# Writing a chunk's residual early, and dropping the join at a chunk's end, in a delta-rule attention and two-MLP kernel

## The chip, the cores and the metric

The kernel runs on one core of a Trainium2 chip. The metric is the device time of one execution in microseconds (us); lower is better.

## The reference

Three parts run one after the other, for 4 batches of 768 tokens.

```python
# 1: attention with the delta rule, 8 heads of 48
k_n = k / (np.linalg.norm(k, axis=-1, keepdims=True) + 1e-06)
for t in range(S):
    y[:, :, t] = einsum('bhd,bhde->bhe', q[:, :, t], state)
    v_old = einsum('bhde,bhd->bhe', state, k_n[:, :, t])
    state = state + beta * einsum('bhd,bhe->bhde', k_n[:, :, t], v[:, :, t] - v_old)
# 2: mixing over tokens, then an MLP (384 -> 1536 -> 384)
u = x + (x.transpose(0, 2, 1) @ U @ V).transpose(0, 2, 1)
x1 = u + np.maximum(u @ w_ch1, 0) @ w_ch2
# 3: 2-D Fourier transform, normalisation, a second MLP of the same size
u = x1 + real(fft(fft(x1, axis=1), axis=2))
out = u + np.maximum(normalise(u) @ w_ch1, 0) @ w_ch2
```

## The kernel before, in words

Attention works on 24 chunks ("units"): 4 batches of 6 chunks of 128 tokens, all 8 heads together. A chunk's own triangular system is prepared without knowing the state (`s_front`, `s_turn`, `s_prep_a`, `s_split`, `s_prep_b`, `s_prep_c`; the last one ends with the copy of the inverse, `nf<-ps_n`). Then `s_solve` walks the chunks in order, since each needs the state that the chunk before left. Within a chunk it writes the scaled values `vt` into the PSUM tile `R` (called `res` in the profile; ScalarE at L1087 or VectorE at L1089), adds state times keys to it with 16 matmuls (`res<-Sst,...`, L1055), and solves in three rounds, each of which reads `R` (`rh<-res`, L1068 or L1070). After the third read come `Ul` (L1121), the state update (`ps_s<-Uh,kb` and so on; `S`, L1135), the copies of the state to two fp16 halves (`Sst`, through L244 and L1145), and the chunk's output (40 matmuls into `ps_s`, then L1142, which overwrites `vt`). At the end stands a join, and the next chunk's write of `R` comes after it. In a batch's first chunk the state is zero and its matmuls are left out.

`s_mixed` adds a finished chunk's output into `hu` (`ps_hu`, L1026) and stores it. `s_mix` builds the first MLP's input once a batch's six chunks are done, with three tiles each for a block of 384 tokens (L1317, L1319, and a transposing DMA at L1338). `s_mlp` is the MLP: `ps_h` (L1190) and `acc` (L1226). The weights arrive as 64-bit numbers, are turned to fp32 on VectorE (L293, L296, L300) and split into two fp16 parts (L365 and L368). Parts 3 and the second MLP follow in `second`, once attention is done; `fold` there prepares the transform's input on GpSimd (L251) and ScalarE (L1451).

No engine chooses at run time: each works through its own list in order. These lists are made beforehand by the planner `Weave`, which keeps a clock for each engine, takes the cost that every step declares, and always issues the step with the smallest sum of earliest start and bias. A step may name two engines, of which the planner takes one by end time with a price on its duration. `PR0` and `MB0` are biases until the first batch's attention is done, `PR`, `MB`, `WB1` those after it, `P2` those of the last part; a more negative bias goes earlier. `MB0` belongs to `s_mix` up to its first finished block, `WB1` to the weights. `UP` is the number of units in which a sum of two matrices is made by one more matmul with the identity (L900) instead of an addition on VectorE. `HB` decides when the small part of an MLP's hidden value is made by a matmul with the identity (L1204) instead of VectorE (L1209). Real waits are semaphores; the planner's join only makes its own clock wait.

Of the kernel before, what the change touches and what calls it, by code (L numbers as in the profile page):

```python
# [15 lines left out]
ALU = mybir.AluOpType  # L16
# [17 lines left out]
NV = 2  # L34
AGE0 = -5
AGE = 16
EPS0 = -1085
FILL = 47
EPS = -309
UP = 13  # L40
UE = 0
NP = 27
GATE = 3
UA = 8
SPARE = 270
SPW = 120
PR0 = (-337, -112, -95, -78, -360, -173, -425, 225)
PR = (-41, -98, -140, -142, 118, 51, -956, -408)
ME = -78
MX = -401  # L50
MB = -515
MB0 = -564
P2 = (-467, -323, -887, -360, -372, -386, -1140, -392)
MP = 39
HB = -550
WB1 = -575
WB = -15
PRICE0 = {'p': 1.0, 'v': 1.45, 'a': 0.71, 'g': 0.38}
PRICE = {'p': 1.0, 'v': 0.29, 'a': 0.22, 'g': 0.14}
PRICE2 = {'p': 1.0, 'v': 283.18, 'a': 3.3, 'g': 1.14}  # L60
SC = 16.0
CQ, CV, CW, CF = 6, 10, 9, 9
CU = 5
# [8 lines left out]
class Weave:  # L72
# [66 lines left out]
    def run(self, streams, until=None):  # L139

        for s in streams:
            if not s.started:
                s.started = True
                self.step(s, None)
        while True:
            if all(s.req is None for s in streams[:until]):
                return
            best, posted, aged, fill = None, len(self.mark), [], []
            first = {}
            for s in streams:  # L150
                if s.req is None:
                    continue
                c = self.pick(s)
                if c is not None and s.fill is not None:
                    fill.append((c, s))
                elif c is not None:
                    rank = c[0] + s.bias[c[2] == "p"] + (self.aging * (s.age - self.oldest) if s.age is not None else 0.0)
                    first[c[2]] = min(first.get(c[2], 1e18), c[0])
                    if best is None or rank < best[0]:
                        best = rank, c, s  # L160
                    if s.age is not None:
                        aged.append((s.age, rank, c, s))
            if len(self.mark) > posted:
                continue
            for c, s in sorted(fill, key=lambda x: x[0][0]):
                if best is None or c[0] <= best[1][0] + 200.0 and c[0] + c[1] <= first.get(c[2], 1e18) + s.fill:
                    best = c[0], c, s
                    break
            assert best is not None, [s.req for s in streams]
            if best[2].age is not None:  # L170
                near = [x for x in aged if x[0] < best[2].age and x[2][2] == best[1][2] and x[1] < best[0] + self.window]
                if near:
                    best = min(near, key=lambda x: x[:2])[1:]
            _, (t, ns, e, mode, x), s = best
            end = t + ns
            self.free[e] = end
            if x in "wg":
                self.port = end
            if mode == "chain":
                s.main, s.par = {e: end} if ns else dict(s.par), {}  # L180
            elif mode == "par":
                s.par[e] = max(s.par.get(e, 0.0), end)
            elif len(s.req) == 3:
                self.dma = max(self.dma, end + self.FETCH) + s.req[2]
                d = {"dma": s.par, "sidedma": s.side, "late": s.late}[mode]
                d["x"] = max(d.get("x", 0.0), self.dma + self.LAND - self.LAT)
            else:
                s.side = {e: end}
            self.step(s, e)
# [8 lines left out]
def _v(n, rate=1):  # L198
    return 67 + n / (0.96 * rate)


def _a(n, psum=False):
    return (51 if psum else 93) + n / 1.2
# [10 lines left out]
class Builder:  # L214
# [822 lines left out]
    def s_solve(self):  # L1037
# [25 lines left out]
        def part(tag):  # L1063

            t = f16t(tag)
            e = yield {"a": _a(n, True), "v": _v(n)}
            if e == "a":
                nc.scalar.activation(out=t, in_=R, func=ACTF.Copy, scale=-1.0 / SC)  # L1068
            else:
                nc.vector.tensor_scalar(out=t, in0=R, scalar1=-1.0 / SC, scalar2=None, op0=ALU.mult)  # L1070
            return t

        def inverse(tag, x):
            ps = work()
            yield from hmm(ps, [(lambda h: Nf[:, h, :], x)])
            t = f16t(tag)
            yield from self.cp(t, ps, n, "chain", psum=True)
            return t

        for u, (b, c) in self.each():  # L1080
            yield ("v", u)
            yield ("scl", b)
            up, sv = self.scl[b]
            vt = self.vt[u]
            e = yield {"a": _a(n) + 94, "v": _v(n)}
            if e == "a":
                nc.scalar.activation(out=R, in_=vt, func=ACTF.Copy, scale=up)  # L1087
            else:
                nc.vector.tensor_scalar(out=R, in0=vt, scalar1=up, scalar2=None, op0=ALU.mult)  # L1089
            yield ("s", u)  # L1090
            un = self.un[u]
            dn = self.ap2.tile([128, 1], F32, tag="dn", name="dn")
            yield {"v": 130}, "par"
            nc.vector.tensor_scalar(out=dn, in0=sv, scalar1=un["sq1"], scalar2=-(2.0 ** -CV), op0=ALU.mult, op1=ALU.mult)
            yield ("c", u)
            yield ("al", 4 * u + 3)
            KT, K2, GPh, GPl, Nf, kb16 = un["KT"], un["K2"], un["GPh"], un["GPl"], un["Nf"], un["kb16"]

            def rest(x):
                return hmm(R, [(lambda h: GPh[:, h, 0:128], x), (lambda h: GPl[:, h, 0:128], x)], [(self.ids, x)],  # L1100
                           start=False)

            if c:
                yield from hmm(R, [(lambda h: KT[:, 0, h, :], St), (lambda h: K2[:, 0, h, :], St)], start=False)
            Rh = yield from part("rh")
            U0 = yield from inverse("U0", Rh)
            yield from rest(U0)
            Rh = yield from part("rh")
            d1 = yield from inverse("d1", Rh)
            yield from rest(d1)  # L1110
            ps = work()
            yield from hmm(ps, [], [(self.id16, U0), (self.id16, d1)], mode="side", stop=False)
            Uh = f16t("Uh")
            yield {"w": _v(n, 2)}, "side"
            nc.vector.tensor_tensor(out=Uh, in0=U0, in1=d1, op=ALU.add)
            Rh = yield from part("rh")
            yield from hmm(ps, [(lambda h: Nf[:, h, :], Rh)], start=False)
            yield "join"
            Ul = f16t("Ul")
            yield {"v": _v(n)}  # L1120
            nc.vector.tensor_tensor(out=Ul, in0=ps, in1=Uh, op=ALU.subtract)  # L1121
            terms = [(lambda h: GPh[:, h, 128:256], Uh), (lambda h: GPl[:, h, 128:256], Uh)]
            if c > 0:
                terms += [(lambda h: KT[:, 1, h, :], St), (lambda h: K2[:, 1, h, :], St)]
            terms.append((lambda h: GPh[:, h, 128:256], Ul))
            if c < NC - 1:
                ps = work()
                yield from hmm(ps, [(lambda h: kb16[:, h, 0, :], Uh), (lambda h: kb16[:, h, 1, :], Uh),
                                    (lambda h: kb16[:, h, 0, :], Ul)], m=64)
                yield {"v": _v(n)}  # L1130
                if c == 0:
                    S32 = self.ap2.tile([64, H, D], F32, tag="S32", name="S32", bufs=1)
                    nc.vector.tensor_scalar(out=S32, in0=ps[0:64], scalar1=1.0 / SC, scalar2=None, op0=ALU.mult)
                else:
                    nc.vector.scalar_tensor_tensor(out=S32, in0=ps[0:64], scalar=1.0 / SC, in1=S32, op0=ALU.mult, op1=ALU.add)  # L1135
            ps = work()
            yield from hmm(ps, terms, mode="side")
            if c < NC - 1:
                St = self.ap2.tile([128, H, D], F16, tag="Sst", name="Sst")
                yield from self.cp(St[0:64], S32, n, "chain")  # L1140
            yield {"a": _a(n, True) + 94}, "side"
            nc.scalar.activation(out=vt, in_=ps, func=ACTF.Copy, scale=dn)  # L1142
            if c < NC - 1:
                yield {"w": _v(n)}
                nc.vector.tensor_tensor(out=St[64:128], in0=S32, in1=St[0:64], op=ALU.subtract)  # L1145
            yield "join"
            self.wv.post("sol", u)
            self.wv.oldest = u + 1

# [603 lines left out]
```

## Time and profile before

| what | before |
|---|---|
| median of 3 runs | 1037.67 us (1035.9 to 1040.18) |
| profiled execution | 1041.91 us, its span 1039.8 us |
| busy share of the span | PE 88%, VectorE 70%, ScalarE 53%, GpSimd 34% |
| mean granted TensorE clock | 0.939 |

PE is TensorE's matmuls, PEld its weight loads, DVE is VectorE, ACT ScalarE, POOL GpSimd, SP the queue that issues most DMAs. A row such as `L1068 ACT ACTIVATE rh<-res` is line 1068 on ScalarE, writing `rh` from `res`. What stands in brackets behind a row of the timeline is the idle time of that engine ahead of the instruction and what ended it.

### The profile page before, as it was taken

The page shows a single profiled execution, that of the slowest core. Times are in us where ns is not written, and L with a number is a line of the kernel's source. Part 1 is how long each engine was busy: PE and PEld are TensorE (multiplying, and loading weights), DVE is VectorE, ACT ScalarE, POOL GpSimd, SP SyncE. Part 2 cuts the span into 40 slices and gives each one's busy share as a digit, 9 for nine tenths or more (in the row PEclk, how much of TensorE's full clock was granted, in tenths as well). Part 3 has the DMA queues.
Part 4 walks back from the last instruction along what each step waited for, and adds up shares of the span by engine and source line. Part 5 has one row for each costly group of instructions (what it writes and reads, how often), then busy time and mean ns, then how long its engine had stood idle before and what let it go on. Part 6 is the DMA issues. An engine that isn't in the chain of part 4 may idle for free. (4 is left out here: it accounts for less than half of the span.)

```text
span 1039.8 us, 25511 instructions
## 1 busy us (share of the span) xinstructions
PE 913.1 (88%) x10282; PEld 622.6 (60%) x10282; DVE 724.9 (70%) x1664; ACT 548.6 (53%) x1358; POOL 352.2 (34%) x330
## 2 busy tenths in 40 slices
PE   3465777589999899999999879999999999999998
PEld 2344665356777666676676546655756665655655
DVE  6898889898898998998765367765735554444532
ACT  5665676767777766667655244447723232222221
POOL 3554244213444323454110360046555532012010
PEclk8575989589999999999999989999999999999999
DMA  6996677316756565543502546522211311202110
GB/s 189 224 219 163 160 183 174 78 39 146 152 133 162 105 151 112 142 109 79 114 25 70 164 105 192 130 87 71 35 54 50 95 28 54 69 24 61 58 34 23
DMA packets 158253, 110.87 MB, mean 107 GB/s; under 512 B 117484, under 2 KB 146424, under 8 KB 158136
## 3 DMA queue, kind: packets, MB, share of 16 engines
q1 hardware_dynamic: 155688, 102.01, 40.6%
q0 software_dynamic: 2448, 7.24, 2.5%
q8 instruction: 80, 1.31, 0.5%
q14 instruction: 37, 0.30, 0.1%
HBM read 55.63 MB, written 14.16 MB: 67 GB/s over the span
## 5 line engine op out<-in xcount | busy, mean ns | idle before, releaser
L1226 PE MATMUL acc<-w2s,hh 128*128 128x384 f16 x1152 | 281.8, 326 | 4.9 <-DVE u L1624 3.1
L1190 PEld LDWEIGHTS <-w1s 128*128 128x128 f16 x1728 | 163.5, 98 | 114.5 <-issue 14.7
L1196 ACT ACTIVATE hh<-ps_h 128x384 f16<-128x384 f32 x192 | 93.7, 488 | 205.6 <-PE ps_h L1190 201.8
L251 POOL TENSOR_TENSOR GPl<-g,GPh 128x512 f16<-128x512 f32 x92 | 116.1, 1262 | 235.1 <-ACT GPh L244 174.2
L1209 DVE SCALAR_TENSOR_TENSOR hl<-ps_h,hh 128x384 f16<-128x384 f32 x147 | 81.6, 555 | 161.6 <-ACT hh L1196 155.8
L1226 PE MATMUL acc<-w2s,hl 128*128 128x384 f16 x576 | 188.1, 327 | 0.2 <-DVE hl L1209 0.2
L1190 PE MATMUL ps_h<-u,w1s 128*128 128x384 f16 x864 | 169.6, 329 | 11.9 <-DVE hl L1209 10.5
L1190 PE MATMUL ps_h<-uh,w1s 128*128 128x384 f16 x864 | 157.9, 327 | 0.0
L1226 PEld LDWEIGHTS <-hh 128*128 128x128 f16 x1152 | 106.2, 98 | 64.8 <-issue 8.0
L902 PEld LDWEIGHTS <-bd 128*128 128x128 f16 x1728 | 71.6, 99 | 45.7 <-issue 18.6
L1226 PEld LDWEIGHTS <-hl 128*128 128x128 f16 x576 | 56.2, 98 | 38.2 <-DVE hl L1209 0.6
L841 DVE TENSOR_TENSOR g<-ps_g,mask 128x512 f32<-128x512 f32 x96 | 65.6, 683 | 12.1 <-PE ps_g L835 11.0
L834 PE MATMUL ps_g<-KT,BT 128*128 128x256 f16 x192 | 54.0, 301 | 10.0 <-ACT t L993 5.0
L244 ACT ACTIVATE GPh<-g 128x512 f16<-128x512 f32 x75 | 47.0, 626 | 28.0 <-DVE g L841 27.3
L251 POOL TENSOR_TENSOR pair<-x1f,pair 128x384 f16<-128x384 f32 x24 | 22.2, 925 | 111.8 <-ACT pair L1594 106.8
L251 POOL TENSOR_TENSOR pm<-xq 97x768 f32<-97x768 f32 (+1 forms) x16 | 29.3, 1850 | 79.5 <-DMA xq<-x1d 72.1
L835 PE MATMUL ps_g<-K,BT 128*128 128x256 f16 x192 | 54.6, 305 | 1.9 <-DMA K<-KT 1.8
L1068 ACT ACTIVATE rh<-res 128x384 f16<-128x384 f32 x63 | 30.5, 484 | 20.0 <-PE res L1055 10.2
L902 PE MATMUL lanes<-R,bd 128*128 128x32 f16 x768 | 34.7, 179 | 4.5 <-ACT R L244 2.9
L882 DVE TENSOR_TENSOR bd<-Xc,mmask 128x1024 f16<-128x1024 f16 x48 | 34.2, 712 | 5.9 <-ACT Xc L936 5.5
L1055 PEld LDWEIGHTS <-GPh 128*128 128x128 f16 x768 | 30.2, 98 | 9.7 <-issue 6.7
L251 POOL TENSOR_TENSOR kb<-kq,rb 128x384 f32<-128x384 f32 x21 | 18.2, 867 | 50.8 <-DVE rb L658 10.9
(270 smaller groups left out, 1866.6 us busy)
## 6 DMA issues: line engine op xcount, KB each, us to landing
wst<-in_moe_w_ch_dram SPq DMA_DIRECT2D x51, 384.0 KB, 3.4
K<-KT SPq DMA_DIRECT2D x46, 256.0 KB, 3.9
kq<-in_k_dram SPq DMA_DIRECT2D x24, 192.0 KB, 3.8
kq<-in_q_dram SPq DMA_DIRECT2D x24, 192.0 KB, 4.2
vt<-in_v_dram SPq DMA_DIRECT2D x24, 192.0 KB, 2.9
xnd<-vt SPq DMA_DIRECT2D x24, 192.0 KB, 3.5
xn<-xnd SPq DMA_DIRECT2D x24, 192.0 KB, 3.0
x1d<-u SPq DMA_DIRECT2D x24, 192.0 KB, 1.9
```

The costliest lines, as they stand in the source:

```text
L244: self.nc.scalar.activation(out=out, in_=in_, func=ACTF.Copy)
L251: (self.nc.vector if eng == "v" else self.nc.gpsimd).tensor_tensor(out=out, in0=in0, in1=in1, op=op)
L834: nc.tensor.matmul(o, BT[:, h, :], KT[:, :, h, :], start=i == 0, stop=False, skip_group_check=True)
L835: nc.tensor.matmul(o, BT[:, h, :], K2[:, :, h, :], start=False, stop=True, skip_group_check=True)
L841: nc.vector.tensor_tensor(out=g32.rearrange("p i (a t) -> p (i a) t", a=2), in0=ps.rearrange("p i (a t) -> p (i a) t", a=2), in1=self.mask ...
L882: self.nc.vector.tensor_tensor(out=dst.rearrange("p h (j c) -> p h j c", j=n), in0=x, in1=mask[:, None, :, :].to_broadcast(shape), op=ALU. ...
L902: nc.tensor.matmul(ps[:, h, :], lhs[:, h, :], rhs[:, h, :], start=plus is None, stop=plus is None or h == H - 1)
L1068: nc.scalar.activation(out=t, in_=R, func=ACTF.Copy, scale=-1.0 / SC)
L1190: nc.tensor.matmul(ps[:, i, :], w[:, k, fs], u[x][:, k, :], start=(m == 0), stop=(m == 3 * KD - 1))
L1196: nc.scalar.activation(out=hh, in_=ps, func=ACTF.Relu, scale=1.0 if wi else 1.0 - 2.0 ** -11)
L1209: nc.vector.scalar_tensor_tensor(out=hl, in0=ps, scalar=0.0, in1=hh, op0=ALU.max, op1=ALU.subtract)
L1226: nc.tensor.matmul(acc, h[:, ds_], w, start=(f == 0 and j == 0), stop=(f == KF - 1 and j == 2))
```

## The change

The write of `R` for the next chunk becomes a function `first`. `s_solve` issues it right after `Ul` of the running chunk, if the planner's clock already has the next chunk's values and scale; otherwise it stays where it was. The join moves from a chunk's end to the place after the first read of the next chunk's `R`. The planner gets a kind of step ("late", without a DMA) whose end only a join waits for. About thirty of the planner's numbers change too.

```diff
-EPS0 = -1085
+EPS0 = -1123
-UP = 13
+UP = 15
-SPW = 120
+SPW = 167
-PR0 = (-337, -112, -95, -78, -360, -173, -425, 225)
-PR = (-41, -98, -140, -142, 118, 51, -956, -408)
-ME = -78
-MX = -401
-MB = -515
-MB0 = -564
-P2 = (-467, -323, -887, -360, -372, -386, -1140, -392)
+PR0 = (-337, -266, -95, -78, -360, -189, -429, 241)
+PR = (-41, -98, -140, -167, 118, 38, -1050, -459)
+ME = -57
+MX = -389
+MB = -494
+MB0 = -626
+P2 = (-467, -323, -722, -360, -372, -386, -1054, -392)
-HB = -550
-WB1 = -575
-WB = -15
-PRICE0 = {'p': 1.0, 'v': 1.45, 'a': 0.71, 'g': 0.38}
+HB = -620
+WB1 = -585
+WB = -12
+PRICE0 = {'p': 1.0, 'v': 1.45, 'a': 0.71, 'g': 0.27}
-PRICE2 = {'p': 1.0, 'v': 283.18, 'a': 3.3, 'g': 1.14}
+PRICE2 = {'p': 1.0, 'v': 446.37, 'a': 7.92, 'g': 0.8}
...
+            elif mode == "late" and len(s.req) == 2:
+                s.late[e] = max(s.late.get(e, 0.0), end)
...
+        def first(u, mode):
+
+            up = self.scl[self.units[u][0]][0]
+            e = yield {"a": _a(n) + 94, "v": _v(n)}, mode
+            if e == "a":
+                nc.scalar.activation(out=R, in_=self.vt[u], func=ACTF.Copy, scale=up)
+            else:
+                nc.vector.tensor_scalar(out=R, in0=self.vt[u], scalar1=up, scalar2=None, op0=ALU.mult)
+
+        ready = None
         for u, (b, c) in self.each():
-            yield ("v", u)
-            yield ("scl", b)
-            up, sv = self.scl[b]
+            if u != ready:
+                yield ("v", u)
+                yield ("scl", b)
+                yield from first(u, "chain")
+            sv = self.scl[b][1]
             vt = self.vt[u]
-            e = yield {"a": _a(n) + 94, "v": _v(n)}
-            if e == "a":
-                nc.scalar.activation(out=R, in_=vt, func=ACTF.Copy, scale=up)
-            else:
-                nc.vector.tensor_scalar(out=R, in0=vt, scalar1=up, scalar2=None, op0=ALU.mult)
...
             Rh = yield from part("rh")
+            yield "join"
             U0 = yield from inverse("U0", Rh)
...
             nc.vector.tensor_tensor(out=Ul, in0=ps, in1=Uh, op=ALU.subtract)
+            if u + 1 < len(self.units):
+                keys = ("v", u + 1), ("scl", self.units[u + 1][0])
+                if all(self.wv.mark.get(x, 1e18) <= self.wv.free["p"] for x in keys):
+                    for x in keys:
+                        yield x
+                    yield from first(u + 1, "late")
+                    ready = u + 1
...
-            yield "join"
             self.wv.post("sol", u)
```

## Rows read from the trace of the kernel before

**Rows 1.** Windows by stage: span, busy us of each engine, granted clock, DMA.
```profile
103.00:182.00 79.00, 57.57 (x1229) 48.23 (x1226) 70.63 (x156) 54.00 (x143) 30.03 (x29) 0.90 0.71 171
182.00:216.00 34.00, 19.94 (x204) 13.82 (x205) 29.08 (x66) 25.42 (x56) 8.46 (x8) 0.55 0.34 77
216.00:575.00 359.00, 341.42 (x5377) 248.95 (x5374) 301.58 (x670) 245.95 (x619) 114.06 (x98) 1.00 0.49 110
720.00:1040.00 320.00, 308.78 (x2009) 192.64 (x2006) 151.68 (x382) 95.53 (x223) 98.19 (x94) 0.99 0.19 51
```

**Rows 2.** Timeline, all engines, chunk 1 to chunk 2: start us, duration us.
```profile
114.37 0.49 PE L1055 MATMUL ps_s<-Ul,GPh 128*128 128x48 f16 x8
...
115.38 0.58 ACT L1087 ACTIVATE res<-vt,sup 128x384 f32<-128x384 f32 x1
...
116.13 0.36 PE L1055 MATMUL res<-Sst,KT 128*128 128x48 f16 x8
```

**Rows 3.** Timeline, all engines, chunk 2 to chunk 3.
```profile
130.41 0.51 ACT L244 ACTIVATE Sst<-S 64x384 f16<-64x384 f32 x1
...
131.93 0.54 DVE L1145 TENSOR_TENSOR Sst<-S,Sst 64x384 f16<-64x384 f32 x1
...
134.55 0.59 ACT L244 ACTIVATE nf<-ps_n 64x512 f16<-64x512 f32 x1
...
135.20 1.49 PE L1026 MATMUL ps_hu<-UU,vt 128*128 128x32 f32 x6 [0.49 <-ACT nf L244]
...
136.50 0.51 PE L1055 MATMUL res<-Sst,KT 128*128 128x48 f16 x8
```

**Rows 4.** Timeline, all engines, chunk 3 to chunk 4.
```profile
150.05 0.55 DVE L1145 TENSOR_TENSOR Sst<-S,Sst 64x384 f16<-64x384 f32 x1
...
151.11 0.36 PE L1055 MATMUL res<-Sst,KT 128*128 128x48 f16 x8
```

**Rows 5.** Timeline, all engines, chunk 4 to chunk 5.
```profile
168.36 0.58 ACT L244 ACTIVATE nf<-ps_n 64x512 f16<-64x512 f32 x1
...
170.27 0.36 PE L1055 MATMUL res<-Sst,KT 128*128 128x48 f16 x8
```

**Rows 6.** Timeline of ScalarE after the first batch's attention.
```profile
198.73 0.60 ACT L1317 ACTIVATE xn<-u,few 128x384 f16<-128x384 f32 x1
...
203.48 0.61 ACT L365 ACTIVATE w1s<-wf,few 128x384 f16<-128x384 f32 x1 [0.53 <-DVE w2s L368]
204.00 0.60 ACT L1317 ACTIVATE xn<-u,few 128x384 f16<-128x384 f32 x1
```

**Rows 7.** Timeline of SP's queue in the same stretch.
```profile
199.00 7.67 SPq L1338 DMA_TRANSPOSE u<-xn  x3
```

**Rows 8.** Timeline of TensorE in the same stretch.
```profile
210.80 1.13 PE L1190 MATMUL ps_h<-u,w1s 128*128 128x384 f16 x3
...
216.51 0.27 PE L900 MATMUL lanes<-R,id 128*128 128x256 f16 x1 [0.23 <-ACT R L244]
216.62 0.35 PE L902 MATMUL lanes<-R,bd 128*128 128x32 f16 x8
```

**Rows 9.** Line 900, one of its two groups of sums.
```profile
L900 PE MATMUL lanes<-Nc,id x26: 269/273/421, 34.2 to 307.2; 128*128 128x256 f16 x26
```

**Rows 10.** Line 1204.
```profile
L1204 PE MATMUL ps_h<-hh,idm x45: 322/323/337, 216.9 to 550.2; 128*128 128x384 f16 x45
```

**Rows 11.** Timeline, all engines, after attention's end.
```profile
600.49 0.94 ACT L1451 ACTIVATE fs<-pm,few 97x772 f16<-97x772 f32 x1 [8.96 <-POOL pm L251]
...
603.48 3.04 PE L1190 MATMUL ps_h<-u,w1s 128*128 128x384 f16 x9 [8.15 <-DVE hl L1209]
```

**Rows 12.** Timeline of SP's queue, the load of chunk 3's values.
```profile
124.97 1.20 SPq L806 DMA_DIRECT2D vt<-in_v_dram  x1
```

**Rows 13.** The same load's line: from issue to landing.
```profile
DMA to landing us min/median/max: 2.4/2.9/3.4
```

**Rows 14.** Waits of SP's queue: total us, times, longest us.
```profile
SPq L806 <- PE lanes L902: 13.2, 10, 4.5
```

## The prediction

> **What bounds the kernel now.** I read the busy shares by slice first, then the same by stage. From about 216 us on TensorE is the bound: it is busy 341.42 of 359 us up to attention's end and 308.78 of 320 us in the last part, at the full clock [rows 1]. Work there can only be shortened by taking matmuls away or by closing the few gaps. Ahead of 216 us it is not the bound: between 103 and 182 us, where chunks 1 to 5 are solved, TensorE is busy 57.57 of 79 us, VectorE 70.63, ScalarE 54.00; between 182 and 216 us, while the first batch's result becomes the MLP's first input, TensorE is busy 19.94 of 34 us [rows 1]. The MLP's first matmul starts at 210.80 [rows 8]. So a microsecond counts if it brings that start forward, since all matmuls behind it are still to be done at one rate; in the 359 us stretch the same saving on the chain of chunks is filled by the MLP's matmuls and buys next to nothing.
>
> Next I read the timeline at each handover from chunk to chunk, and asked what stood last ahead of the 16 matmuls that add the state to `R`; then the timeline of the 182 to 216 stretch on ScalarE, SP's queue and TensorE; and last the waits and the timeline after attention's end, where the one large hole in TensorE's work lies.
>
> **The handovers.** No instruction is removed or added by the early write: all 24 writes of `R` stay, at 0.58 us on ScalarE [rows 2]. They move past the state's copies, the output's 40 matmuls and L1142, and no DMA moves with them. What is saved is what stood between the state and the first matmul on `R`.
> - Chunk 1 to 2: the output's last matmuls end at 114.37 + 0.49 = 114.86, the write of `R` fills 115.38 to 115.96, and the matmuls on `R` start at 116.13 [rows 2]. They could start at 114.86: 1.3 us.
> - Chunk 2 to 3: here `R` is not last. The inverse of chunk 3 is copied until 134.55 + 0.59 = 135.14, TensorE then does `ps_hu` for chunk 2's output, and the matmuls on `R` start at 136.50 [rows 3]. Without the join they can come ahead of `ps_hu`, though the planner still waits for the inverse: 136.50 - 135.14 = 1.4 us.
> - Chunk 3 to 4: the state's second half ends at 150.05 + 0.55 = 150.60 and the matmuls start at 151.11 [rows 4]: 0.5 us.
> - Chunk 4 to 5: the inverse ends at 168.36 + 0.58 = 168.94 and the matmuls start at 170.27 [rows 5]: 1.3 us.
>
> The sum is 4.5 us. From below it is 0: at chunk 3 the inverse ends 2.7 us after the state's second half (131.93 + 0.54 = 132.47) [rows 3], and if VectorE, busy 70.63 of 79 us, sets the pace of that, a shorter chain only waits longer for the next inverse. From above, if the inverse comes earlier too (the bias of `s_prep_c` falls from -112 to -266), the 2-to-3 handover could follow the state's first half at 130.92 [rows 3] and give 5.6 in place of 1.4: 8.7 us in all. I take 4.5, since the rows give it one by one and the bias of `s_prep_c` works against a late inverse.
>
> The later 18 handovers are costed at nothing: the cover is TensorE's MLP work, 95% busy. With that cover gone they would be worth about 1.1 us each, the mean of the four.
>
> **From the sixth chunk to the MLP.** `MB0` falls from -564 to -626 and `WB1` only from -575 to -585, so of a mix step and a weight step that could start at the same time the weight went first by 11 and now the mix goes first by 41. The place to see it is ScalarE: the second tile of the MLP's input is scaled at 198.73, the third only at 204.00, with four weight splits of about 0.6 us between (the last at 203.48), beside four steps of attention [rows 6]. SP's three transposes of these tiles take 7.67 us for the same reason [rows 7], and the MLP starts after the third. Without the four splits the third tile is 4 x 0.6 = 2.4 us earlier. Bounds: 0, if the order there is set by SP's queue and not by the bias, and 204.00 - 199.33 = 4.7, if nothing stands between. I take 2.4. The splits put off are needed only as the MLP gets to them, and ScalarE has 25.42 of 34 us busy there [rows 1].
>
> **What TensorE gets more of.** `UP` from 13 to 15 gives two units four more identity matmuls each. One half of those now there is 26 in number [rows 9], which is 13 units times two. From one to the next instruction such a matmul takes 216.62 - 216.51 = 0.11 us at the full clock [rows 8], so 8 x 0.11 = 0.9 us, in the stretch where TensorE is the bound; eight additions leave VectorE for it. `HB` from -550 to -620 lets more of the 45 identity matmuls of the MLP in [rows 10], at an estimated 0.11 x 384 / 256 = 0.165 us each. How many is not seen: from 0 to 10 more is 0 to 1.7 us. I take 0, since neither engine's load changes there. The other biases and prices move choices between engines that I cannot see; GpSimd's price in the first stage falls and could relieve VectorE. I take 0, within 2 us either way.
>
> **The hole after attention.** TensorE waits 8.15 us for VectorE until 603.48; behind that is ScalarE, which stood 8.96 us for GpSimd's folding (L1451) with the MLP's `hh` queued behind it [rows 11]. The new `P2` shifts only the mix and the last output, so I expect the hole again. Bounds: all of it gone, 8.15 us gained; or another like it elsewhere, 8.15 us lost.
>
> **The sum.** 1041.9 - 4.5 - 2.4 + 0.9 = 1035.9 us against the profiled execution's own 1041.91. That one is 0.41% above the median of the runs, so scaled to the median: 1035.9 x 1037.67 / 1041.91 = 1031.7 us, which is 0.6% below before.
>
> **The rivals.**
> 1. *The preparation sets the pace.* VectorE's 70.63 of 79 us [rows 1] and the inverse of chunk 3 that ended after the state [rows 3] speak for it; chunks 2 and 4, where the write of `R` came last [rows 2, 4], speak against it. Then the handovers give 0 to 1.5, the order 0 to 2, and TensorE takes 0.9 more: 1035 to 1038.5, no change that can be told. It covers the case that the early write isn't made at all because the planner's clock lacks the values.
> 2. *The early write blocks its engine.* The values of chunk 3 are requested at 124.97 [rows 12] and land 2.4 to 3.4 us later [rows 13], by 128.4; the copy of the state that the early write now stands ahead of starts at 130.41 [rows 3]. That leaves 2.0 us, less the write's own 0.58. The request itself waits in SP's queue up to 4.5 us [rows 14]. Once a landing is later than planned by more than 1.4 us, the state's copy waits for it, and from 1.4 + 1.1 us on the handover loses more than it saves. At 4.5 us late it loses 2 us instead of gaining 1.1; in all four handovers that is +8 in place of -4.5: 1037.67 + 8 - 2.4 + 0.9 = 1044 us. That an engine stands still with ready work behind the waiting step is seen in this trace: ScalarE for 8.96 us with `hh` behind [rows 11]. By the Trainium skill ("PSUM — Partial Sum Buffer", section "Engine vs sequencer instructions") the queues of ScalarE and VectorE are strict first-in first-out, so nothing behind an early write could overtake it; the 8.96 us row agrees. Against it: the planner asks for the load's planned landing ahead of time, and later chunks have their values earlier still.
> 3. *The new order closes the hole after attention* (or most of it): 1031.7 - 8 = 1023.7. Its price is sure [rows 11], but nothing in the diff aims at it.
> 4. *The new order opens another such hole*: 1031.7 + 8 = 1040, and with rival 1 1044. A hole of that size stands in the order of before, which shows that the planner's clock can be 8 us off.
>
> **How the numbers follow.** My forecast has 0.42, rival 1 0.33, rival 2 0.09, rival 3 0.08, rival 4 0.08. A difference under 0.5% (5.2 us) is about what a measurement of this kernel can't tell from no change: below 1032.5 is faster, above 1042.9 slower. The forecast's own spread (handovers 0 to 8.7, mix 0 to 4.7, the rest within 2) lies mostly at 1026 to 1035, so about 0.4 of the whole falls below 1032.5 with it, and with rival 3 0.48. Slower are rival 2 and half of rival 4 with its neighbours: 0.15. The rest, 0.37, is no change. For the range I leave out the far ends of rivals 2 to 4: 1021 to 1043.
>
> **What would show it.** Right: the matmuls on `R` follow the output's last matmuls or the inverse by under 0.3 us at chunks 2 to 5, with the write of `R` ahead of the state's copies; the first `ps_h` near 204 us in place of 210.8; 60 identity matmuls on L900; the 8 us hole still there. Wrong: chunk 5's last output no earlier than before though each handover is shorter (rival 1: look for where the inverse ends); ScalarE or VectorE idle ahead of an early write with a load as its releaser (rival 2); a TensorE hole of several us gone or new behind 575 us (rivals 3, 4). A first `ps_h` that starts earlier with the same end would show that the bound behind it is not TensorE's work, and the whole sum would be wrong.

## The result: slower, and the profile after

The changed kernel takes 1047.89 us (median of 4 runs, 1047.39 to 1048.78), the kernel before beside it 1038.75 (4 runs): a ratio of 1.0086, 95% interval 1.0071 to 1.0101. It is about 9 us slower. The forecast was 1031.7 us with a range of 1021 to 1043: wrong in its direction, and outside the range.

The windows by stage of the changed kernel, in the columns of [rows 1]:

```profile
103.00:182.00 79.00, 59.85 (x1061) 48.85 (x1061) 68.26 (x151) 54.30 (x141) 31.10 (x30) 0.70 0.68 168
182.00:216.00 34.00, 18.83 (x181) 12.15 (x179) 28.75 (x57) 27.23 (x60) 12.01 (x11) 0.55 0.32 71
216.00:575.00 359.00, 334.93 (x5333) 244.30 (x5331) 301.95 (x648) 240.50 (x611) 108.73 (x99) 1.00 0.50 113
720.00:1040.00 320.00, 314.00 (x2041) 195.47 (x2040) 153.27 (x389) 94.68 (x219) 97.92 (x93) 0.99 0.20 52
```

Against [rows 1], TensorE is busy 6.5 us less between 216 and 575 us and 5.2 us more in the last part: it works later what it did not do in the long middle. What comes ahead of the MLP did not make the kernel late: the MLP's first matmul starts at 208.5 us, 2.3 us earlier than before [rows 8]. The gain is small, though: by 255 us 77 of the matmuls into `ps_h` have started, against 75.

The profiled execution of before was 3 us above the median; a second one, e3_before_again below, is nearer (one run, 1038.91 us, span 1036.8). The changed kernel's profiled run took 1047.6 us, span 1045.8. The next two views count the MLP's `ps_h` matmuls alone. In each: span, busy us and count on TensorE, VectorE and ScalarE, granted clock, DMA. First the second profile of before, then the changed kernel:

```profile
216.00:255.00 39.00, 13.98 (x67) 0.00 (x0) 6.81 (x14) 1.00 0.40 79
255.00:293.00 38.00, 11.17 (x53) 0.00 (x0) 4.90 (x10) 1.00 0.71 157
293.00:345.00 52.00, 15.12 (x68) 0.56 (x1) 6.33 (x13) 1.00 0.57 130
345.00:410.00 65.00, 21.00 (x103) 0.54 (x1) 9.24 (x19) 1.00 0.64 141
```

```profile
216.00:255.00 39.00, 13.73 (x67) 0.00 (x0) 5.82 (x12) 1.00 0.42 89
255.00:293.00 38.00, 9.21 (x44) 0.00 (x0) 3.87 (x8) 1.00 0.67 145
293.00:345.00 52.00, 14.73 (x69) 0.56 (x1) 6.37 (x13) 1.00 0.61 143
345.00:410.00 65.00, 17.42 (x81) 0.55 (x1) 7.28 (x15) 1.00 0.60 135
```

A matmul on a border counts in both windows. Taken as one window, 216 to 410 us, the changed kernel has 257 of them, the kernel before 287; the same view of `acc` gives 225 and 252. These 57 matmuls follow each other 0.16 us apart where nothing waits: 9.1 us of the MLP, and the lag arises in two stretches, 255 to 293 and 345 to 410 us. Attention ends earlier instead (last chunk at 562.1 us against 574.8). The lag has the size of the whole loss, but it is not the loss: run g2 below, before with one number changed, is as far behind at 410 us (259 and 228; `ps_h`, then `acc`) and only some 2 us slower.

```profile
216.00:410.00 194.00, 56.22 (x259) 0.56 (x1) 25.25 (x52) 0.99 0.59 130
216.00:410.00 194.00, 48.25 (x228) 3.63 (x6) 0.99 0.59 130
```

What TensorE waited for between 216 and 410 us (total us, times, longest us), the second profile of before and then the changed kernel:

```profile
PE ps_u L1305 <- DVE g L841: 3.0, 5, 1.4
PE lanes L902 <- DVE bd L882: 2.4, 5, 1.2
PE ps_h L1190 <- ACT hl L1206: 1.3, 1, 1.3
```

```profile
PE lanes L904 <- DVE bd L884: 3.8, 5, 1.6
PE ps_h L1220 <- ACT hh L1212: 1.1, 3, 0.6
PE lanes L904 <- DVE R L914: 1.0, 1, 1.0
PE lanes L904 <- ACT R L246: 1.0, 1, 1.0
```

In this window TensorE's idle times over 0.05 us grew from 10.9 to 16.0 us in all, and most of that is the inverse's (`lanes`; `bd` is an operand that VectorE makes for it): 2.8 us became 6.2. Two of these waits are shown whole below, under the last experiments.

The saving at the handovers was there and then gone. Chunk 3 ends at 144.6 us, 5.6 us earlier than before; chunk 4 at 169.1, 0.6 us later; chunk 5 at 182.7, 0.7 later. The timeline of the changed kernel from chunk 3 to 4 (VectorE; ScalarE; TensorE):

```profile
145.16 0.62 DVE L1162 TENSOR_TENSOR Sst<-S,Sst 64x384 f16<-64x384 f32 x1
...
144.04 0.56 ACT L1159 ACTIVATE vt<-ps_s,dn 128x384 f32<-128x384 f32 x1
...
147.23 0.58 ACT L1087 ACTIVATE res<-vt,sup 128x384 f32<-128x384 f32 x1
...
152.68 0.59 ACT L246 ACTIVATE nf<-ps_n 64x512 f16<-64x512 f32 x1 [1.00 <-PE ps_n L1002]
...
151.58 0.50 PE L408 MATMUL ps_k<-wf 128*128 128x128 bf16 x3 [1.07 <-DVE wf L302]
...
153.62 0.42 PE L837 MATMUL ps_g<-K,BT 128*128 128x256 f16 x1
153.83 0.53 PE L1057 MATMUL res<-Sst,KT 128*128 128x48 f16 x8
```

The state is ready at 145.16 + 0.62 = 145.78, the inverse of chunk 4 only at 152.68 + 0.59 = 153.27: the matmuls on `R` start behind that, at 153.83, which is 8.05 us after the state where it was 0.51 in [rows 4]. TensorE's list itself stood 1.07 us for a weight ahead of the inverse's last product.

The write of `R` is not early here. It stands at 147.23 on ScalarE's list, behind the end of chunk 3 at 144.04. It is early from chunk 2 to 3, where it starts at 124.00 and the matmuls on `R` follow the state's second half by 0.05 us. In 10 of the 23 handovers, from chunk 3 to 4, 4 to 5 and 5 to 6 among them, it stands behind the old chunk's last instruction on its engine, as before the change: the planner's clock did not yet have the next chunk's values and scale.

After attention the hole is there again, in two parts: TensorE waits 3.30 and 7.14 us, and ScalarE stands for GpSimd's folding as in [rows 11] (ScalarE; TensorE; the last row is TensorE in the second profile of before):

```profile
586.37 0.94 ACT L1467 ACTIVATE fs<-pm,few 97x772 f16<-97x772 f32 x1 [7.45 <-POOL pm L253]
...
572.18 1.62 PE L1206 MATMUL ps_h<-u,w1s 128*128 128x384 f16 x9 [3.30 <-DVE hl L1225]
...
588.99 3.04 PE L1206 MATMUL ps_h<-u,w1s 128*128 128x384 f16 x9 [7.14 <-DVE hl L1225]
...
601.67 2.98 PE L1190 MATMUL ps_h<-u,w1s 128*128 128x384 f16 x9 [6.02 <-DVE hl L1209]
```

Behind the 3.30 us nine matmuls take 1.62 us, behind the 7.14 us 3.04: the clock is granted at half there, 0.50 between 585 and 590 us and 0.59 between 590 and 595. In the second profile of before it is 0.66 between 600 and 605 us and full again behind that.

### The profile page after: what moved, and what is told of

Same layout as the page of the kernel before. It is cut to its first block, busy times and chain, and to the rows that moved or that the text cites. A ratio compares the mean times of both kernels' runs of the same rounds, so it can differ in the third digit from the quotient of the medians.

```text
span 1045.8 us, 25561 instructions
## 1 busy us (share of the span) xinstructions
PE 923.4 (88%) x10289; PEld 628.2 (60%) x10289; DVE 733.0 (70%) x1650; ACT 554.8 (53%) x1372; POOL 348.7 (33%) x332
## 4 chain that ended last, share of the span: by engine, by line
PE 61%; DVE 18%; DMA 7%; ACT 7%; issue 4%; POOL 2%; SPq 1%; DVEq 0%; ACTq 0%; POOLq 0%
PE ps_h L1206 22%; PE acc L1242 21%; PE ps_s L1057 3%; DVE g L843 2%; PE lanes L904 2%; DMA sqn<-in_v_dram 2%; DVE bd L884 2%; DMA K<-KT 2%; PE ps_d L1501 2%; PE res L1057 1%; POOL pm L253 1%; PE ps_hu L1028 1%; PE ps_q L1523 1%; PE ps_g L837 1%; PE ps_g L836 1%
## 5 line engine op out<-in xcount | busy, mean ns | idle before, releaser
L253 POOL TENSOR_TENSOR GPl<-g,GPh 128x512 f16<-128x512 f32 x93 | 113.3, 1218 | 178.1 <-ACT GPh L246 153.0
L246 ACT ACTIVATE GPh<-g 128x512 f16<-128x512 f32 x80 | 50.1, 626 | 18.5 <-DVE g L843 17.9
L373 POOL TENSOR_TENSOR w1s<-wf,w1s 128x384 f16<-128x384 f32 x16 | 14.6, 913 | 99.7 <-ACT wf L372 99.5
L884 DVE TENSOR_TENSOR bd<-Xc,mmask 128x1024 f16<-128x1024 f16 x48 | 36.9, 770 | 3.6 <-ACT Xc L938 3.3
```

Source lines behind the costliest of these rows:

```text
L246: self.nc.scalar.activation(out=out, in_=in_, func=ACTF.Copy)
L253: (self.nc.vector if eng == "v" else self.nc.gpsimd).tensor_tensor(out=out, in0=in0, in1=in1, op=op)
L884: self.nc.vector.tensor_tensor(out=dst.rearrange("p h (j c) -> p h j c", j=n), in0=x, in1=mask[:, None, :, :].to_broadcast(shape), op=ALU. ...
```

## The experiments

All ratios are to the kernel before on the same chip, with the 95% interval.

**Code and numbers apart.** e1 is the changed code with all old numbers, e2 the old code with all new numbers (24 values), e3 the kernel before once more, e4 the moved join alone with old numbers:

```
-            if u + 1 < len(self.units):
+            if False and u + 1 < len(self.units):
```

> The changed code (early write of the residual, join moved) with every planner number of the kernel before. Theory A (the code itself costs: attention is planned ahead of the MLP and the MLP's blocks fall behind): slower than before by 5 to 10 us, about 1044 to 1049, with block 3 of the first MLP ending 10 us or more later than before's 537.9 us. Theory B (the new numbers cost, the early write is a small gain): 1034 to 1039 us. Theory C (any new order of this planner lands within some 10 us of the old one, whatever it is for): anything from 1030 to 1050, with no pattern shared with the other runs.

> The code of before with all of the new planner numbers. Theory A: within 4 us of before. Theory B: slower by 6 to 12 us, 1045 to 1051, with the same late MLP blocks as the changed kernel (block 2 ending near 473 us in place of 454.8). Theory C: anything from 1030 to 1050.

> The kernel before, unchanged, for a second profile of it. All theories: 1036 to 1040 us. Its profiled execution of before was 3 us above the median of the runs; if a second profile is nearer to the median, the stretch in which it differs from the first tells how much of a difference between two profiles is chance (expected: the granted clock ahead of 216 us).

> The old numbers and the join moved, but no early write: the next chunk's residual is written where it was. Theory A with the join as its cause: slower by 4 to 10 us, like the code alone. Theory A with the early write as its cause, or theory B: within 3 us of before. Theory C: anything from 1030 to 1050.

Measured: e1 1064.52 us, 1.0249 [1.0226, 1.0272]; e2 1068.25, 1.028 [1.0257, 1.0304]; e4 1051.65, 1.013 [1.0107, 1.0152]. Each half alone loses far more than both together. The MLP's first matmul starts at 236.5 us in e1 (25.7 later than before, the time 27 us longer), at 224.9 in e4 (14.1 and 14), at 226.4 in e2 (15.6 and 31). So a late start of the MLP is paid nearly in full in e1 and e4; e2 loses half of its time elsewhere. In e4 the chain first runs ahead: chunk 4 ends at 161.4 us, 7 us earlier than before. Then TensorE's list stands, and the inverse of chunk 5 ends at 179.8 us (168.9 before). TensorE in e4, and two windows of the same stretch:

```profile
164.42 0.35 PE L980 MATMUL ps_z<-xm,nf 128*128 128x32 f16 x8 [2.81 <-ACT ssc L629]
...
168.04 0.40 PE L837 MATMUL ps_g<-K,BT 128*128 128x256 f16 x1 [2.52 <-DMA K<-KT]
```

```profile
160.00:170.00 10.00, 3.38 (x46) 2.40 (x43) 7.93 (x18) 5.30 (x13) 6.10 (x7) 0.80 0.89 175
170.00:180.00 10.00, 7.77 (x115) 6.29 (x115) 8.66 (x20) 5.67 (x15) 4.29 (x4) 0.50 0.59 146
```

TensorE is busy 3.38 of 10 us, and in the next 10 us its clock is granted at half. Taking the join away does shorten the chain; what comes due next is the preparation.

**The early write alone.** g1 keeps the lists of TensorE, GpSimd and SyncE of before and only puts the write of `R` on ScalarE right behind the write of `Ul`, in 22 of the 23 handovers, whether or not the values are there in time. The write at the old place is left out for these (not shown):

```
...
+            if u + 1 < len(self.units) and u + 1 in self.vt and self.units[u + 1][0] in self.scl:
+                nc.scalar.activation(out=R, in_=self.vt[u + 1], func=ACTF.Copy, scale=self.scl[self.units[u + 1][0]][0])
+                ready = u + 1
```

> The kernel before with its order kept: TensorE, GpSimd and SP have the very same lists, and only the writes of the residual are issued earlier, on ScalarE, right after Ul wherever the next chunk's values are already requested (the planner still books them at the old place). It is the idea of the change without a new plan. Prediction's handover terms (1.3 + 0.5 us where the write came last, nothing where TensorE's own order or the inverse sets the start): 0 to 3 us below before, 1034.5 to 1038. Rival 2 (the early write blocks ScalarE until its values land): 3 to 8 us above before, with ScalarE idle ahead of L1127 and a DMA as releaser.

Measured: 1040.47 us, 1.0019 [1.0001, 1.0036]. `R` is ready 5 to 7 us ahead of the matmuls on it in chunks 2 to 5, yet these start at 115.89, 136.13, 153.14 and 172.22 us, against 116.13, 136.50, 151.11 and 170.27 before: TensorE's own order decides, and at chunks 4 and 5 they are 2 us later. There the early write blocks its engine (ScalarE; TensorE):

```profile
147.63 0.58 ACT L1127 ACTIVATE res<-vt,sup 128x384 f32<-128x384 f32 x1 [2.36 <-DMA vt<-in_v_dram]
148.24 0.59 ACT L993 ACTIVATE t<-ps_x 64x512 f16<-64x512 f32 x1
...
165.63 0.58 ACT L1127 ACTIVATE res<-vt,sup 128x384 f32<-128x384 f32 x1 [4.16 <-DMA vt<-in_v_dram]
...
148.88 0.44 PE L1000 MATMUL ps_n<-nf,t 128*64 128x64 f16 x8 [1.50 <-ACT t L993]
```

ScalarE stands 8.5 us in four such waits for the values. A step of the next inverse (`t<-ps_x`) comes behind the write, and TensorE waits 1.50 us for it. In the changed kernel no write of `R` waits for the load of its values.

**Single numbers.** f1 is before with `MB0` -626; g2 before with `UP` 15; f2 the changed kernel with `UP` 13.

> The kernel before with one number changed: MB0 from -564 to -626, so that mix steps go ahead of weight steps between the first batch's end and the first MLP block. It is the prediction's second term by itself. If that term is right: the third L1317 some 2 us or more earlier than 204.0, the first ps_h at 206 to 209 us in place of 210.8, and the time 1.5 to 4 us lower (1034 to 1036). Rival (SP's queue or the tile's readiness sets it, not the bias): the first ps_h within 0.5 us of 210.8 and the time within 1.5 us of before.

> The kernel before with UP = 15 alone, so that the plan is made anew from chunk 13's preparation on and eight more identity matmuls run. Theory of the price: 0.5 to 1.5 us above before (8 x 0.11 = 0.9). Theory C (any new plan of the main stage costs several us, since the old numbers fit the old plan): 4 to 15 us above before.

> The changed kernel with UP back at 13, all else new. Theory of the price (the eight more identity matmuls are TensorE work in the stretch where it is the bound): 0.5 to 3 us below the changed kernel's 1048. Theory C (every order that the planner makes anew from one number costs or gains several us by chance): a change of over 4 us in either direction, with MLP blocks ending at other times from about 290 us on.

Measured: f1 1038.94 us, 1.0008 [0.9993, 1.0024]; g2 1039.84, 1.0015 [0.9999, 1.0032]; f2 1054.8, 1.0169 [1.0136, 1.0202]. In f1 the order changes in one pair on SyncE only, and the third tile still comes 5.28 us behind the second:

```profile
197.88 0.60 ACT L1317 ACTIVATE xn<-u,few 128x384 f16<-128x384 f32 x1
...
203.16 0.60 ACT L1317 ACTIVATE xn<-u,few 128x384 f16<-128x384 f32 x1
```

In f2 less work for TensorE (the identity matmuls of two units) costs 7 us more: a hole of 8.02 us opens at 721.78.

**Parts of the changed kernel.** f3 is the changed kernel with the old main-stage numbers (`UP`, `PR`, `ME`, `MX`, `MB`, `HB`, `WB1`); f4 with early write and moved join in the first six chunks only; h3 with old `PR` alone; h4 with old `ME`, `MX`, `MB` alone.

> The changed kernel with the old numbers of the stage after the first batch (PR, ME, MX, MB, HB, WB1, UP), the new ones ahead of it. Theory D (the first batch is in order in the changed kernel, and the 9 us are lost after 216 us through the new numbers of that stage): near before, 1034 to 1042. Theory E (lost there through the early write, or because code and numbers belong together): 1046 or more. First ps_h near 208 us in either.

> The changed kernel, but the early write and the moved join only for the first batch's six chunks; from the seventh on the handover is that of before. All numbers new. Theory E with the early write as the cause in the later batches: 1036 to 1044, and MLP block 2 ending near 455 us rather than 473. Theory D: within 4 us of 1048. Theory C: anything from 1038 to 1065.

> The changed kernel with the old due times of the preparation in the main stage (PR) alone. If the loss between 257 and 410 us comes from when the preparation of a chunk is due, the attention ends later, the lag there goes, and the time is 1038 to 1042 us. If no single number makes the loss, it is anything from 1042 to 1056.

> The changed kernel with the old numbers ME, MX and MB (the lead of mix and its bias against the MLP) alone. If these make the loss between 257 and 410 us, the time is 1038 to 1042 us; if no single number makes it, anything from 1042 to 1056.

Measured: f3 1043.39 us, 1.004 [1.0021, 1.0059]; f4 1047.3, 1.009 [1.0065, 1.0115]; h3 1063.81, 1.0248 [1.0211, 1.0284]; h4 1041.56, 1.003 [1.001, 1.005]. f4 is level with the changed kernel, so nothing points to the later 18 chunks' early write and join as the cause. Putting back all old numbers of the main stage takes away half of the loss (f3, 1047.9 - 1043.4 = 4.5 us), putting back `ME`, `MX`, `MB` alone some 6 us (h4, 1047.9 - 1041.6). From 216 us on TensorE's idle times over 0.05 us sum to 33.2 us in h4 and in g2, as in the second profile of before (36.0 in the first), and to 39.2 in the changed kernel. h4 does not close the gap at 410 us (in one window from 255 to 410 us it has 192 `ps_h` matmuls, the changed kernel 192, before 222); it is the hole after attention that shrinks, from 3.30 + 7.14 to 1.94 us:

```profile
586.04 1.62 PE L1206 MATMUL ps_h<-u,w1s 128*128 128x384 f16 x9 [1.94 <-DVE hl L1225]
```

h3 is level with before up to about 600 us and then stands 18.89 us at 724.92, ahead of the second MLP's first matmul.

**The hole after attention.** g3 and g4 are the kernel before, with the planner told that GpSimd's first folding ends 8 and 12 us later:

```
+            if b == 0 and i == 0:
+                main = self.wv.cur.main
+                main["g"] = main.get("g", 0.0) + 8000.0
```

> The kernel before; in the last part the planner is told that GpSimd's first folding for batch 0 ends 8 us later, so that ScalarE's fs<-pm goes behind some of the MLP's hh. All work is the same, and the plan is the old one up to attention's end. If the hole after attention is ScalarE's list waiting for the folding with hh behind it: the hole shrinks from 6 to 8 us to under 2, and the time falls by 3 to 8 us, to 1030 to 1035. If a new plan opens holes elsewhere (theory C): 1036 to 1046, and where the hole went is to be seen.

> As the run before it with 12 us in place of 8. Hole theory: also without the hole, the same time within 2 us as with 8. Theory C: a time that differs from the one with 8 us by 3 us or more.

Measured: g3 1057.26 us, 1.0191 [1.0162, 1.0219]; g4 1056.2, 1.0183 [1.0152, 1.0214]. In g3 the hole breaks into 2.96, 1.45 and 4.39 us, and a larger one opens:

```profile
738.35 2.08 PE L1190 MATMUL ps_h<-uh,w1s 128*128 128x384 f16 x6 [11.61 <-DMA uh<-pair]
```

**Why the inverse is late: VectorE beside GpSimd.** The longest waits of the changed kernel for `bd` stand at 393.82 (1.64 us) and 275.65 (1.10). `GPh` and `GPl` are the high and low half of a Gram matrix `g`; GpSimd forms `GPl`. Timelines of VectorE, GpSimd and TensorE at the two places:

```profile
272.18 1.20 DVE L1162 TENSOR_TENSOR Sst<-S,Sst 64x384 f16<-64x384 f32 x1 [0.23 <-ACT Sst L246]
...
274.43 1.67 DVE L884 TENSOR_TENSOR t<-Tc,mmask 128x1024 f16<-128x1024 f16 x1
276.01 0.68 DVE L884 TENSOR_TENSOR bd<-GPh,mmask 128x1024 f16<-128x1024 f16 x1
...
391.26 1.64 DVE L884 TENSOR_TENSOR bd<-GPh,mmask 128x1024 f16<-128x1024 f16 x1
392.93 1.15 DVE L1162 TENSOR_TENSOR Sst<-S,Sst 64x384 f16<-64x384 f32 x1
394.12 1.29 DVE L884 TENSOR_TENSOR bd<-Xc,mmask 128x1024 f16<-128x1024 f16 x1
...
271.81 1.16 POOL L253 TENSOR_TENSOR GPl<-g,GPh 128x512 f16<-128x512 f32 x1 [5.92 <-ACT GPh L246]
274.39 1.16 POOL L253 TENSOR_TENSOR GPl<-g,GPh 128x512 f16<-128x512 f32 x1 [1.42 <-DVE Tc L949]
...
391.19 1.16 POOL L253 TENSOR_TENSOR GPl<-g,GPh 128x512 f16<-128x512 f32 x1 [0.40 <-ACT GPh L246]
...
276.75 0.36 PE L904 MATMUL lanes<-mmask,bd 128*128 128x32 f16 x8 [1.10 <-DVE bd L884]
...
395.46 0.37 PE L904 MATMUL lanes<-Nc,bd 128*128 128x32 f16 x8 [1.64 <-DVE bd L884]
```

An instruction of line 884 takes 0.68 us; started 0.04 or 0.07 us behind a GpSimd instruction it takes 1.67 and 1.64. GpSimd ends at 274.39 + 1.16 = 275.55, VectorE 0.55 us later at 276.10: it looks as if VectorE did not begin until GpSimd was done. At the second place three long instructions stand in a row, and TensorE waits for the last, which ends at 395.41. To test it, h1 and h2 let GpSimd write zeros where it forms `GPl`, in before and in the changed kernel, with every other engine's list in the same order, so that the low half is left out of the result there; i1 writes the zeros twice; i2 forms `GPl` on VectorE. The edit of h1 and h2:

```
-                    yield from self.sub(gl, g32, gs, 512)
+                    e = yield {"w": _v(512), "g": _g(512)}, "chain"
+                    if e == "g":
+                        nc.gpsimd.memset(gl, 0.0)
+                    else:
+                        self.tt(e, gl, g32, gs, ALU.subtract)
```

> The kernel before, but where GpSimd forms the low half of a Gram matrix (GPl, 128x512, 1.16 us, 93 times in the changed kernel) it writes zeros instead, so that it reads nothing there; the low half is thus left out of the result for these. Order of TensorE, VectorE, ScalarE and SyncE as before. If VectorE's two-input instructions are stretched because GpSimd works on SBUF beside them, few of them stay stretched between 216 and 575 us (in the kernel before 24 instructions by 15 us in all), and the time falls by 2 to 8 us. If the stretching costs nothing behind 216 us since TensorE is covered, the time stays within 2 us of 1038.7.

> The changed kernel with the same edit (zeros in place of the low half where GpSimd forms it). Theory stretch: the 9 us that the changed kernel loses arise where stretched VectorE instructions of the inverse come late for TensorE (275.65 and 393.82 us in its profile), so that this run comes within 4 us of the kernel before with the same edit. Rival order: the new list of TensorE places inverse and MLP worse whatever the durations are; it then stays 7 to 11 us behind that one. Half way would mean both.

> As the kernel before without the reads (h1), but GpSimd writes the zeros twice, so that it is as long at work as with the difference (about 1.05 instead of 1.16 us), and still reads nothing there. If it is GpSimd's reads that stretch VectorE's instructions, the time stays near h1's 1021.7 us, at most 4 us above. If the 16 us came from GpSimd being done sooner, it goes back to 1031 us or more.

> The kernel before, complete, with the low half of the Gram matrix formed on VectorE at the place where GpSimd formed it (93 instructions of 128x512 at about 0.7 us more on VectorE, 65 us), all other lists in the same order. If the stretching is dearer than the work, the time falls below 1035 us; if VectorE's in-order list now waits for ScalarE's high half and the 65 us are paid, it rises to 1045 us or more.

Measured: h1 1021.74 us, 0.9834 [0.9799, 0.987]; h2 1031.67, 0.9939 [0.9916, 0.9961]; i1 1026.32, 0.9886 [0.985, 0.9923]; i2 1057.5, 1.02 [1.017, 1.023]. Both kernels gain 16 us, and 10 us stay between them: whatever the reads cost, they cost it alike in both, so the theory that stretched instructions make the difference falls, and the new order is what is left. With GpSimd at work as long as before and not reading (i1), 10 us of the gain remain, 4.6 us less than in h1, a little outside the 4 expected. GpSimd's zeros also don't wait for `GPh`, so `GPl` is ready sooner; no run shows how much of the 10 or 16 us is that and how much is the stretching. Moved to VectorE (i2), the work costs about 21 us: its place on GpSimd is right in this kernel.

## Why the prediction was wrong, step by step

- *The handovers (4.5 us).* The saving came and was given back: 5.6 us at the end of chunk 3, -0.6 at chunk 4, by the inverse of chunk 4. Chunk 5 ends 0.7 us later than before, the sign that was named for rival 1, which had a third of the chance. The early write itself is worth nothing (g1), and the planner made it in only part of the handovers; the moved join does the shortening (e4).
- *The mix ahead of the weights (2.4 us).* Refuted: `MB0` changes nothing there (f1). The MLP started 2.3 us earlier, where the two steps together were to give 6.9.
- *`UP` (0.9 us).* The count is right: 60 in the two groups of sums as forecast, 84 in all against 76; alone (g2) it measured 1.0015 [0.9999, 1.0032], some 2 us and not told from nothing. `HB` at nothing: 45 became 44.
- *The hole after attention stays.* It stayed and grew: 3.30 + 7.14 = 10.4 us, against 6.02 and 8.15 us in the two profiles of before. The prediction looked at `P2` alone for it; h4 shows that `ME`, `MX` and `MB` move it.
- *The failed step* is "from about 216 us on TensorE is the bound", with "the other biases and prices move choices between engines that I cannot see ... I take 0, within 2 us either way". The MLP's start was earlier, as said, and the end was 9 us later. A stage in which TensorE is 95% busy gives no cover to a new order, since the order sets the other 5%. The runs that put back main-stage numbers in the changed kernel show the size of what was taken as 2: -4.5 us (f3), -6 (h4), +7 (f2, `UP`) and +16 (h3, `PR`).
- Where the 9.0 us between the two spans lie: from 216 us on TensorE is idle 39.2 us against 33.2 (gaps over 0.05 us), 6.0 more, and busy 786.9 us against 783.9, 3.0 more. Of the idle time 4.4 us are the larger hole after attention; without it, 3.3 more lie ahead of 575 us and 1.6 fewer behind. Against the first profile of before, whose hole is 8.15 us, the idle time is 3.2 us more, so one profile of each says this to some 3 us only. Of the busy time the eight identity matmuls are an estimated 0.9 us. TensorE works at half clock for 5.1 us behind its hole, against 2.8, and half of the difference is an estimated 1.2 us. The last 0.9 us stay open. So does why these numbers make that order: the runs show which group of numbers carries how much, not which instruction's place.
- Rival 4 (another hole, 1040 to 1044 us) was nearest to the end, with a hole that grew and many small ones in the place of a new one. Rival 2, an engine blocked behind an early write, doesn't show in the changed kernel, whose planner writes early only with the values there. Its mechanism is real: in g1 ScalarE stood up to 4.16 us for the values. The price was small, 0.2% of the time.

## What to carry to other kernels

Where a planner writes the order, a small change of code is a change of the whole order, and numbers tuned to one code are not those of the other: price it by runs of code and numbers apart, and keep a few per cent of both signs in the range. Shortening a chain helps until the next supply (here the inverse) is due, so look for its end first. A count of matmuls that lags in the middle is no loss by itself (g2): compare idle and busy time to the end. A hole is closed only if the work that is then early has what it needs: f2, g3, g4 and h3 each opened one of 8 to 19 us near 725 us.

## What the runs showed of the hardware

VectorE's instructions with two inputs in SBUF wait for GpSimd's that read it. In the second profile of before, 32 TENSOR_TENSOR instructions of VectorE between 100 and 575 us take over 0.25 us more than the median of their line, 22.6 us together. Each of the 32 starts beside a GpSimd instruction that is under way and ends behind it, those of line 882 always by 0.55 us. In h1 9 do, by 4.6 us, and in i1 10, by 5.8, each beside a GpSimd instruction that still reads and none beside the zeros alone. VectorE's `g<-ps_g,mask`, one of whose inputs is in PSUM, is not stretched:

```profile
L841 DVE TENSOR_TENSOR g<-ps_g,mask x96: 622/685/693, 20.8 to 524.5; 128x512 f32<-128x512 f32 x96
```

24 of these 96 start with over 0.6 us of a GpSimd TENSOR_TENSOR still to run, and none takes over 0.69 us. Without the reads of `GPl` the kernel is 1.7% faster in the same order. By the Trainium skill ("SBUF — State Buffer", section "Who interferes with whom") a VectorE instruction with two SBUF inputs contends with a GpSimd instruction that reads SBUF, not with one that only writes it, and the port pair that the two share is an exclusive lock. The rows at 274.39 and 391.19 us and the runs h1 and i1 agree with it.
